# Top-k attention and a low-rank mixer: weighted values of two steps formed together at every other step, with a third buffer for transposed probabilities

## The chip, the cores and the metric

The kernel runs on one core of one Trainium2 chip. The core has five engines that run side by side: TensorE (PE, the matrix array; its weight loads are shown apart as PEld), VectorE (DVE), ScalarE (ACT), GpSimd (POOL) and SyncE (SP, which here issues the DMA transfers). The metric is the device time of one execution in microseconds. The kernel before takes 1774.49 us, the median of three runs from 1774.05 to 1775.44; the profiled execution has a span of 1773.6 us.

## The reference

Attention over 8 batches, 8 heads, 576 rows and a head dimension of 64 keeps the 32 largest scores of each row; its output goes through a low-rank mixer along the sequence and a two-layer MLP. All of it is float32.

```python
scores = scale * np.matmul(q, k.transpose(0, 1, 3, 2))
kth = np.partition(scores, -top_k, axis=-1)[..., -top_k:-top_k + 1]
scores = np.where(scores >= kth, scores, -1000000000.0)
attn = np.exp(scores - np.max(scores, axis=-1, keepdims=True))
attn = attn / (np.sum(attn, axis=-1, keepdims=True) + 1e-09)
x = np.matmul(attn, v)        # then heads side by side: (8, 576, 512)
h = x.transpose(0, 2, 1) @ U @ V
u = x + h.transpose(0, 2, 1)
out = u + np.maximum(u @ w_ch1, 0.0) @ w_ch2
```

U is 576 x 32 and V 32 x 576; w_ch1 is 512 x 2048 and w_ch2 2048 x 512.

## The kernel before

**Tiles and steps.** Heads go in pairs: 4 pairs a batch, 32 pairs g in all. The 576 rows of a pair make five chunks: t = 0 to 3 are 128 rows of both heads, and t = 4 holds the last 64 rows of both heads stacked. One chunk is one step, so step n = 5g + t runs from 0 to 159, and the loop goes on to n = 161 to finish.

**What happens to a chunk.** `scores` (L320 for t = 4, L333 otherwise) forms the scores on TensorE; ACT copies them to the tile Ssb. `front` runs on DVE: it alternates MAX8 (L385, L399) and MATCH_REPLACE8 (L395) to find the 32nd largest score. GpSimd and ACT push the smaller scores far down (L402 and L403, or L419 to L421), and `weigh` (L351) writes the exponentials to E. The chunk's E must then be turned, so that its rows lie along the free dimension, into the tile PT. `turns` does it by transposes on TensorE (L474, L479) with ACT copies (L475, L480). From chunk 30 on (`shared`), the second head of the chunks t < 4 takes another way, `blocks`: a DVE transpose of 32 x 32 blocks (L446), a DMA to DRAM (L452) and back into PT (L456). `values` (L508 and L512, or L498 for t = 4) multiplies PT by the pair's values into a PSUM tile O, which ACT copies to XT (L521), or scales into x for t = 4 (L506). In L508 the stationary operand is 128x128, with the last 64 rows of both heads on a diagonal; in L512 it is 128x64, and the two heads write the two halves of O. In L333 the two heads use the two halves of the array's rows. In L498 the stationary operand is PT itself, 128x128.

**After the last chunk of a pair.** `mixed` transposes XT (L533), applies the row sums, and forms the low-rank products (L544, L556, L558). It is a generator that goes on by one piece with each `fill()`; after the last pair of a batch it puts that batch's MLP, `mlp(b)`, into `fillers`.

**What sets the order.** The order of work on TensorE, ACT, DVE and GpSimd is the order in which the program is written; no planner moves it. In step n from 21 on, the loop issues in turn: the transposes of chunk n-2 between the first four `fill()` calls, the values of chunk n-2, the scores of chunk n+1, and four more `fill()` calls, with pieces of `front` for chunk n and `blocks` for chunk n-1 between. Each `fill()` adds a fixed share to `due` and then takes matmuls of the MLP (L581 and L600) from `fillers` until `due` is paid; if `fillers` is empty, `due` is set to zero. The share is one MLP's work spread over the calls of four head pairs, times `SHORT` in steps with t = 4, times `EARLY` up to step 42. What is left at the end of the loop is run in the last `while` loop.

```python
share = MLP_WORK / (NPAIR * SLOTS * (NT + SHORT))
due += share * (SHORT if t == NT else 1) * (EARLY if n <= 2 * ALONE + 2 else 1)
```

**Buffers.** PT has two buffers of 4.5 KB a partition. The tile hT (two ReLU outputs of one MLP part) has `HT` = 10 buffers of 2.5 KB; one part of an MLP, 320 or 256 columns, fills eight. PSUM tiles of transposes, O, and the mixer's products share a ring of two buffers, `ps_t`; scores have two in `ps_s`, MLP products two in `ps_m`.

Of the kernel before, what the change touches and what calls it, by code (L numbers as in the profile page):

```python
# [8 lines left out]
F32 = mybir.dt.float32  # L9
# [17 lines left out]
def kernel(  # L27
# [30 lines left out]
    P = 128  # L58
# [4 lines left out]
    NT, TAIL = 4, 64  # L63
# [6 lines left out]
    CH = NT + 1  # L70
    ALONE = NPAIR * CH
# [2 lines left out]
    NV = 3  # L74

    BLK = 32
    HT = 10
    PE, ACT = mybir.EngineType.PE, mybir.EngineType.Activation
    DVE, POOL = mybir.EngineType.DVE, mybir.EngineType.Pool

# [2 lines left out]
    attn = ctx.enter_context(tc.tile_pool(name="attn", bufs=2))  # L83
# [45 lines left out]
    def cols(t):  # L129
        return slice(t * P, t * P + rows(t))  # L130
# [4 lines left out]
    def half(h):  # L135
        return slice(h * D, (h + 1) * D)
# [226 lines left out]
    def eased(g, t):  # L363
        return bool(ways(g, t)[2])
# [69 lines left out]
    def shared(g, t):  # L434


        return t < NT and g * CH + t >= ROUNDED

    def blocks(g, t):


        E2 = probs[g, t]
        PT = attn.tile([P, 2 * NT + 1, P], F32, tag="PT", name="PT")
        PTs[g, t] = PT
        y = attn.tile([P, 4, NT, BLK], F32, tag="y", name="y", bufs=1)
        nc.vector.transpose(  # L446
            y.rearrange("p r c j -> p c r j"),
            E2[:, S + TAIL : 2 * S].rearrange("p (c r j) -> p c r j", c=NT, r=4),
        )
        away = dram.tile([P, 4, P], F32, tag="away", name="away")  # L450
        for a in range(4):
            nc.sync.dma_start(  # L452
                away[:, a].rearrange("(r i) n -> i r n", r=4),
                y[a * BLK : (a + 1) * BLK].rearrange("i r c j -> i r (c j)"),
            )
        nc.sync.dma_start(  # L456
            PT[:, NT : 2 * NT].rearrange("p a n -> p (a n)"), away.rearrange("p a n -> p (a n)")
        )

    def turns(g, t):  # L460


        E2 = probs.pop((g, t))
        nh = 2 if t < NT else 1
        if shared(g, t):
            PT = PTs[g, t]
        else:
            PT = attn.tile([P, 2 * NT + 1, P], F32, tag="PT", name="PT")
            PTs[g, t] = PT
        for h in range(1 if shared(g, t) else nh):  # L470
            tp = ps_t.tile([P, NT, P], F32, tag="tp", name="tp")
            for j in range(NT):
                a = h * (S + TAIL) + j * P
                nc.tensor.transpose(tp[:, j, :], E2[:, a : a + P], ident)  # L474
            nc.scalar.copy(PT[:, NT * h : NT * h + NT], tp)  # L475
            yield
        tp = ps_t.tile([P, P], F32, tag="tp", name="tp")
        a = MAIN if nh == 2 else S - P
        nc.tensor.transpose(tp, E2[:, a : a + P], ident)  # L479
        nc.scalar.copy(PT[:, NT * nh], tp)  # L480
        yield

    def inverse(g, lo, hi):
        den = dens[g][:, lo:hi]
        if g == NPAIR - 1:
            nc.vector.tensor_scalar_add(den, den, 1e-9)
        nc.vector.reciprocal(den, den)

    def values(g, t):

        PT = PTs.pop((g, t))
        va, vd, vt = (a[g % NV] for a in (vas, vds, vts))
        O = ps_t.tile([P, P], F32, tag="tp", name="O")
        if t == NT:
            den, x = dens[g], xs[g % 2]
            inverse(g, 2 * NT if g == NPAIR - 1 else 0, 2 * NT + 1)
            for j in range(NT + 1):
                nc.tensor.matmul(  # L498
                    O,
                    lhsT=PT[:, j],  # L500
                    rhs=va[:, :, j, :] if j < NT else vt,
                    start=(j == 0),
                    stop=(j == NT),
                )
            for h in range(2):
                nc.scalar.mul(x[half(h), NT, half(h)], O[half(h), half(h)], den[half(h), 2 * NT :])  # L506
            return
        nc.tensor.matmul(O, lhsT=vd, rhs=PT[:, 2 * NT], start=True, stop=False)  # L508
        PB = PT[:, NT : 2 * NT].rearrange("p a (c j) -> p c a j", c=NT) if shared(g, t) else None
        for j in range(NT):  # L510
            for h in range(2):
                nc.tensor.matmul(  # L512
                    O[half(h)],
                    lhsT=va[:, h, j, :],
                    rhs=PB[:, j] if h and shared(g, t) else PT[:, NT * h + j],
                    start=False,
                    stop=(j == NT - 1),
                )
        if t == 0:
            XTs[g] = attn.tile([P, MAIN], F32, tag="XT", name="XT")  # L520
        nc.scalar.copy(XTs[g][:, cols(t)], O)  # L521
# [49 lines left out]
    def mlp(b):  # L571
# [3 lines left out]
        for chunks, (lo, hi) in zip(PARTS, SPAN):  # L575
            w = hi - lo
            hTs = []
            for f in range(NF):
# [11 lines left out]
                if f % 2 == 0:  # L590
                    hT = mlpp.tile([P, 2, WIDE], F32, tag="hT", name="hT", bufs=HT)
                    hTs += [hT[:, 0], hT[:, 1]]
# [73 lines left out]
    STEPS = NP * CH  # L666
# [4 lines left out]
    fillers, mixing, due = [], [], 0.0  # L671
# [29 lines left out]
    for n in range(STEPS + 2):  # L701
        g, t = divmod(n, CH)
        if n < STEPS:
            if t == 0 and g + 1 < NP:
                load(g + 1)
            if t == 1 and g + 1 < NP:
                ready = prep(g + 1)
            fronts[n] = front(g, t)
            next(fronts[n])
        here, last = fronts.get(n, iter(())), fronts.pop(n - 1, iter(()))  # L710
        if n >= ALONE - 1 and n <= ALONE:

            if n < ALONE:
                next(last)
                values(*divmod(n - 3, CH))
                list(turning)
                next(here)
                next(last)
                scores(*divmod(n + 1, CH))
                values(*divmod(n - 2, CH))  # L720
            list(turns(*divmod(n - 1, CH)))
            values(*divmod(n - 1, CH))
            if n < ALONE:
                next(here)
                next(here)
                inverse(g, 0, 2 * NT)
                mixing.append(mixed(g, 1))
                fill()
                next(here)
                continue  # L730
            fill()
            scores(*divmod(n + 1, CH))
            next(here)
            while mixing:
                fill()
            next_params(1)
            fill()
            next(last, None)
            next(here)
            fill()  # L740
            next(here)
            next(here)
            fill()
            continue
        ease = eased(*divmod(n - 1, CH))
        if n < ALONE:
            if ease:
                next(last, None)
            scores(*divmod(n + 1, CH))
            if n >= 3:  # L750
                values(*divmod(n - 3, CH))
                if (n - 3) % CH == NT:
                    mixing.append(mixed((n - 3) // CH, 3))
            list(turning)
            fill()
            next(here)
            if t < NT:
                next_params(1)
            fill()
            next(ready, None)  # L760
            next(here)
            next(last, None)
            fill()
            next(here)
            if t in (0, 1):
                next_params(1)
            next(here)
            fill()
            if n >= 1:
                turning = turns(*divmod(n - 1, CH))  # L770
            continue
        away = n <= STEPS and shared(*divmod(n - 1, CH))
        if ease:
            next(last, None)
        fill()
        next(turning, None)
        fill()
        next(turning, None)
        if away:
            next(last)  # L780
        fill()
        next(turning, None)
        fill()
        if ease:
            next(last, None)
        if n - 2 >= ALONE:
            values(*divmod(n - 2, CH))
        if n + 1 < STEPS:
            scores(*divmod(n + 1, CH))
        next(here, None)  # L790
        next_params(1)
        if n - 2 >= ALONE and (n - 2) % CH == NT:
            mixing.append(mixed((n - 2) // CH, 5))
        fill()
        next(here, None)
        if away:
            blocks(*divmod(n - 1, CH))
        fill()
        if n <= STEPS:
            turning = turns(*divmod(n - 1, CH))  # L800
        fill()
        next(here, None)
        next(ready, None)
        if t in (1, 3):
            next_params(1)
        next(here, None)
        fill()
# [33 lines left out]
```

## Time and profile before

| | kernel before |
|---|---|
| median of 3 runs | 1774.49 us |
| span of the profiled execution | 1773.6 us |
| PE busy | 1669.3 us, 94% |
| DVE busy | 1560.3 us, 88% |
| ACT busy | 1029.4 us, 58% |
| POOL busy | 846.8 us, 48% |
| mean granted TensorE clock | 0.968 |
| 20 steps in the steady stage | 200.6 us |

A row of the table is the time in which an engine had at least one instruction running. Matmuls overlap, so a matmul's own duration in the profile is longer than its share of TensorE's time; what counts is the distance from one matmul's start to the next one's. The span has three parts: up to 250 us the weights are unpacked beside the first chunks; from 450 to 1620 us the steps repeat with a period of five; after 1633 us, when the last chunk is done, the rest of the MLP work runs by itself. A line of the timeline reads: start in us, length in us, engine, line, operation, output <- inputs, array shape (rows * columns used), moving operand, count, and in brackets the idle time before it with what ended it. A line of the chain of waits reads: start, length, engine, output, line, count.

### The profile page before, as it was taken

How to read it: one execution, taken by the hardware profiler on the slowest of the kernel's cores; microseconds unless marked ns; L12 is line 12 of the kernel's file. 1: busy time of each engine (PE TensorE's matmuls, PEld its weight loads, DVE VectorE, ACT ScalarE, POOL GpSimd, SP SyncE). 2: the span in 40 equal slices, each digit the busy share in tenths (PEclk: the TensorE clock that was granted, in tenths of full speed). 3: DMA queues.
4: the chain of work that ended last, by engine and by line, in shares of the span. 5: the costliest groups of instructions: out<-in, count | busy, mean ns of one | idle time of the engine just before them, and what ended most of it. 6: DMA issues, size and time to landing. Idle time of an engine off the chain costs nothing.

```text
span 1773.6 us, 28992 instructions
## 1 busy us (share of the span) xinstructions
PE 1669.3 (94%) x9851; PEld 1257.5 (71%) x9851; DVE 1560.3 (88%) x3106; ACT 1029.4 (58%) x2682; POOL 846.8 (48%) x591
## 2 busy tenths in 40 slices
PE   4666789999999999999999999999999999999999
PEld 2434556677777877788777877788777877788677
DVE  7999989899999999999999999999999999994000
ACT  4778777555656656565656656565656656564100
POOL 4777677535354554545445454444445444453000
PEclk7687799999999999999999999999999999999999
DMA  3222332222223332222233232232233232211010
GB/s 95 88 82 73 88 85 61 50 59 71 58 67 80 66 72 56 67 68 64 64 71 79 62 70 62 65 70 63 63 73 80 59 73 60 53 50 45 4 15 13
DMA packets 275829, 112.79 MB, mean 64 GB/s; under 512 B 173920, under 2 KB 260192, under 8 KB 275680
## 3 DMA queue, kind: packets, MB, share of 16 engines
q1 hardware_dynamic: 274624, 110.68, 26.4%
q8 instruction: 77, 1.26, 0.3%
q14 instruction: 72, 0.59, 0.1%
q10 hardware_dynamic: 1056, 0.26, 0.1%
HBM read 74.15 MB, written 36.70 MB: 63 GB/s over the span
## 4 chain that ended last, share of the span: by engine, by line
PE 75%; DVE 16%; POOL 4%; ACT 3%; issue 2%; DMA 1%; SPq 0%; POOLq 0%; DVEq 0%
PE mm L581 25%; PE mm L600 24%; DVE rr L395 7%; PE sc L333 6%; PE O L512 6%; DVE m L399 6%; PE tp L474 3%; DVE first L385 2%; PE sc L320 2%; PE O L498 2%; PE up L556 1%; PE O L508 1%; POOL E L402 1%; PE up L558 1%; PE tp L648 1%
## 5 line engine op out<-in xcount | busy, mean ns | idle before, releaser
L399 DVE MAX8 m<-rr 128x8 f32<-128x576 f32 x864 | 614.7, 748 | 5.5
L600 PE MATMUL mm<-hT,w 128*128 128x256 f32 (+1 forms) x2048 | 547.4, 410 | 0.0
L581 PE MATMUL mm<-uT,w 128*128 128x256 f32 (+1 forms) x2048 | 541.5, 410 | 0.9 <-ACT hT L593 0.9
L402 POOL TENSOR_SCALAR E<-Ssb,m 128x576 f32<-128x576 f32 x127 | 281.1, 2214 | 411.7 <-DVE m L399 409.1
L581 PEld LDWEIGHTS mm<-uT,w 128*128 128x128 f32 x2048 | 371.7, 190 | 115.1 <-issue 26.0
L600 PEld LDWEIGHTS mm<-hT,w 128*128 128x128 f32 x2048 | 368.3, 190 | 106.8 <-issue 22.5
L395 DVE MATCH_REPLACE8 rr<-m,rr 128x576 f32<-128x576 f32 x576 | 427.2, 742 | 0.0
L421 POOL TENSOR_TENSOR Ssb<-Ssb,E 128x576 f32<-128x576 f32 x159 | 225.4, 1418 | 122.3 <-ACT E L420 121.7
L351 ACT ACTIVATE E<-Ssb,nmax 128x576 f32<-128x576 f32 x288 | 223.3, 776 | 52.4 <-POOL Ssb L403 34.9
L593 ACT ACTIVATE hT<-mm 128x320 f32<-128x320 f32 (+1 forms) x256 | 105.1, 411 | 240.4 <-PE mm L581 240.1
L385 DVE MAX8 first<-Ssb 128x8 f32<-128x576 f32 x288 | 203.3, 742 | 31.4 <-ACT Ssb L346 31.4
L395 DVE MATCH_REPLACE8 rr<-first,Ssb 128x576 f32<-128x576 f32 x288 | 211.8, 742 | 0.0
L403 POOL TENSOR_TENSOR Ssb<-Ssb,E 128x576 f32<-128x576 f32 x127 | 179.3, 1412 | 10.6
L333 PE MATMUL sc<-qkT 64*128 64x288 f32 x1024 | 170.6, 454 | 6.7 <-ACT Ssb L344 5.8
L474 PE MATMUL tp<-ident,E 128*128 128x128 f32 x736 | 116.0, 283 | 37.1 <-ACT XT L521 14.6
L512 PE MATMUL O<-PT,va 128*64 128x128 f32 x2048 | 146.3, 284 | 1.9 <-DMA PT<-away 1.9
L474 PEld LDWEIGHTS tp<-ident,E 128*128 128x128 f32 x736 | 92.1, 145 | 68.7 <-ACT XT L521 16.6
L475 ACT COPY PT<-tp 128x512 f32<-128x512 f32 x184 | 106.6, 585 | 49.0 <-PE tp L474 46.4
L512 PEld LDWEIGHTS O<-PT,va 128*64 128x64 f32 x2048 | 113.7, 140 | 19.0 <-DMA PT<-away 2.9
L420 ACT ACTIVATE E<-Ssb,least 128x576 f32<-128x576 f32 x159 | 123.3, 776 | 5.2
L333 PEld LDWEIGHTS sc<-qkT 64*128 64x128 f32 x1024 | 93.3, 198 | 45.3 <-issue 14.3
L613 DVE TENSOR_TENSOR oT<-uT,mm 128x320 f32<-128x320 f32 (+1 forms) x8 | 3.6, 455 | 137.1 <-PE mm L600 137.1
(81 smaller groups left out, 1574.0 us busy)
## 6 DMA issues: line engine op xcount, KB each, us to landing
away<-y SPq DMA_DIRECT2D x416, 64.0 KB, 1.8
PT<-away SPq DMA_DIRECT2D x104, 256.0 KB, 2.8
raw<-in_moe_w_ch_dram SPq DMA_DIRECT2D x32, 512.0 KB, 3.8
va<-in_v_dram SPq DMA_DIRECT2D x64, 128.0 KB, 2.3
out_dram<-ob SPq DMA_DIRECT2D x57, 128.0 KB, 2.2
ld<-in_q_dram SPq DMA_DIRECT2D x108, 64.0 KB, 2.4
ld<-in_k_dram SPq DMA_DIRECT2D x108, 64.0 KB, 2.4
ld<-in_q_dram SPq DMA_DIRECT2D x108, 8.0 KB, 2.2
```

Of the source, the lines that this page charges most:

```text
L333: nc.tensor.matmul(sc[:, h, 0:HALF], lhsT=qkT[half(h), 0, cols(t)], rhs=qkT[half(h), 1, i * HALF : (i + 1) * HALF], start=True, stop=True,)
L351: nc.scalar.activation(E, chunk, AF.Exp, bias=nmax, scale=SCALE, accum_out=total)
L385: nc.vector.max(ms[c], curs[c])
L395: nc.vector.match_replace(nxt, ms[c], curs[c], NEG)
L399: nc.vector.max(ms[c], curs[c])
L402: nc.gpsimd.tensor_scalar(Es[c], chunks[c], ms[c][:, 7:8], NEG, ALU.is_lt, ALU.mult)
L403: nc.gpsimd.tensor_tensor(chunks[c], chunks[c], Es[c], ALU.add)
L421: nc.gpsimd.tensor_tensor(chunks[c], chunks[c], Es[c], ALU.subtract)
L474: nc.tensor.transpose(tp[:, j, :], E2[:, a : a + P], ident)
L512: nc.tensor.matmul(O[half(h)], lhsT=va[:, h, j, :], rhs=PB[:, j] if h and shared(g, t) else PT[:, NT * h + j], start=False, stop=(j == NT ...
L581: nc.tensor.matmul(ph[:, 0:w], lhsT=w1[:, cc, f * P : (f + 1) * P], rhs=uT[:, cc, lo:hi], start=(cc == 0), stop=(cc == NC - 1),)
L600: nc.tensor.matmul(po[:, 0:w], lhsT=w2[:, f, c * P : (c + 1) * P], rhs=hTs[f][:, 0:w], start=(f == 0), stop=(f == NF - 1),)
```

## The change

Chunks are weighted in twos. At an even step the loop now forms the values of chunks n-3 and n-2, one after the other; at an odd step it forms none. Scores keep their place, once a step, behind the values. When a pair's last chunk is odd, its `mixed` is thereby put on the list one step later. A chunk's PT now has to live one step longer, so PT gets a third buffer; HT falls from 10 to 8, which gives back the space.

```diff
-    HT = 10
+    HT = 8
...
-        PT = attn.tile([P, 2 * NT + 1, P], F32, tag="PT", name="PT")
+        PT = attn.tile([P, 2 * NT + 1, P], F32, tag="PT", name="PT", bufs=3)
...
-            PT = attn.tile([P, 2 * NT + 1, P], F32, tag="PT", name="PT")
+            PT = attn.tile([P, 2 * NT + 1, P], F32, tag="PT", name="PT", bufs=3)
...
-        if n - 2 >= ALONE:
-            values(*divmod(n - 2, CH))
+
+        weighted = [n - 2] if n > STEPS else [m for m in (n - 3, n - 2) if n % 2 == 0 and m >= ALONE]
+        for m in weighted:
+            values(*divmod(m, CH))
         if n + 1 < STEPS:
             scores(*divmod(n + 1, CH))
         next(here, None)
         next_params(1)
-        if n - 2 >= ALONE and (n - 2) % CH == NT:
-            mixing.append(mixed((n - 2) // CH, 5))
+        for m in weighted:
+            if m % CH == NT:
+                mixing.append(mixed(m // CH, 5))
```

## Prediction

> **What bounds the kernel now.** I read the page first, then the busy time by stretches, the chain of work that ended last inside one steady stretch, the waits, and last the timeline around the one place where TensorE pauses. From the page:
>
> ```profile
> PE 1669.3 (94%) x9851; PEld 1257.5 (71%) x9851; DVE 1560.3 (88%) x3106; ACT 1029.4 (58%) x2682; POOL 846.8 (48%) x591
> ...
> PE 75%; DVE 16%; POOL 4%; ACT 3%; issue 2%; DMA 1%; SPq 0%; POOLq 0%; DVEq 0%
> ```
>
> Shares over the whole span mix stages, so the next view is busy time by stretch (length, then PE, PEld, DVE, ACT, POOL; then granted clock):
>
> ```profile
> 440.00:450.00 10.00, 8.08 (x48) 5.89 (x47) 9.93 (x22) 4.84 (x14) 4.05 (x4) 0.83 0.43 102
> ...
> 700.00:900.00 200.00, 199.83 (x1215) 152.46 (x1214) 193.47 (x384) 119.57 (x318) 95.94 (x64) 1.00 0.30 67
> ```
>
> From 450 to 1620 us TensorE is busy without a gap and DVE has 3% to spare. The list of waits has none of TensorE's between 500 and 1600 us; DVE's own there are 15.9 us for score copies. So in the steady stage the time is the sum of what TensorE's instructions take, and a thing is worth only what it adds to or takes from that sum. The chain there (start, length, what; L600 is the second MLP product, L474 and L479 transposes, L508 and L512 weighted values, L333 scores):
>
> ```profile
> 913.51 0.54 PE mm L600 x2
> 914.05 0.11 PE tp L479
> 914.16 1.08 PE mm L600 x4
> 915.24 0.22 PE O L508 x2
> 915.46 1.03 PE O L512 x16
> 916.49 1.17 PE sc L333 x8
> 917.66 3.43 PE mm L600 x12
> ```
>
> Four L600 take 1.08, so one 320-column matmul 0.27 us; one of 128 columns 0.11 (L479, or L508 x2 in 0.22). L512 fills half the array's columns and runs in pairs: 16 make 8 pairs, 8 x 0.11 = 0.87, but they take 1.03. L333 fills half the rows: 4 pairs of 288 columns at 0.27 x 288/320 = 0.24 make 0.97, but they take 1.17. Twelve L600 after them should take 3.23 and take 3.43. So each group that begins or ends with another shape of array use carries 0.16 to 0.20 us extra, three times a step.
>
> **What the Trainium skill says.** "TensorEngine Tiling (Array Packing)", Tiling Modes, Key Properties: changing the tiling mode, not merely the tile, drains TensorE. The chain agrees: the extra stands where 128x128 meets 128x64, 128x64 meets 64x128, and 64x128 meets 128x128; L600 to L508, both 128x128, pays nothing. "TensorE: Matmul & The Clock Gate", Part 2, Step-by-step: weight loads are pulled ahead of running matmuls, while matmuls keep program order. That fits the 0.27 and 0.11 inside a mode, where no load shows; the part of the extra after a switch is about one load that nothing covers. Same page, Part 1: after an idle window of about 3.4 us the clock falls to half. Here a pause of 1.92 us was followed by a clock of 0.83 in the stretch above. "Perfetto Trace Analysis", Tensor Engine Instruction: matmul ends are estimated, so I used distances between starts.
>
> **The change part by part.** *Order of values.* Before, step n does V (values of n-2), then S (scores of n+1). After, an even step does V(n-3), V(n-2), S, and an odd step S alone. Products, bytes and copies stay the same. Modes, with full for 128x128: V is full (L508) then 64 columns (L512); S is row mode. Two steps before: full, col, row, full, col, row, full: 6 switches. Two steps after: full, col, **full, col**, row, full, then full, row, full: 7. The second L508 puts the array back to full width between the two L512 groups. That is one extra switch, from L512 into L508. Its price from the nearest rows: 0.16 (L512 into L333, exit and half of a short load) to 0.20 (L333 into L600, whose weights are 128 wide as L508's are). I take 0.20. For V of t=4 (L498, all full): pair (t=3, t=4) also has one extra, L512 into L498; pair (t=4, t=0) has none, as L498 to L508 keeps full mode. Even steps from 46 to 160 are 58; step 160 has no S and comes out even, and 11 are (4,0) pairs. 46 x 0.20 = **9.2 us**, all on the path, as nothing else bounds this stage. At 0.16 it is 7.4. The earlier ten pairs lie where TensorE pauses anyway (step 42, below) and are counted at nothing.
>
> *When an MLP opens.* An MLP is handed out by fill() once mixed() has finished the batch's last head pair. That pair's last V is m = 19, 39, 59 ...: always odd, so it moves from step m+2 to m+3, and every MLP from the second on opens eight fill calls later. Does the stock last? One MLP is 144 units (a unit is 512 columns of one product). A call asks 0.9677 units (0.629 for t=4): 36.0 per five steps, and 0.91 of it up to step 42. From step 20: four calls 3.5, steps 21 to 24 25.7, steps 25 to 39 98.3, steps 40 and 41 14.1: 141.6. The rest, 2.4, is gone in the third call of step 42. mixed() needs nine calls from its first. Before, these are calls 5 to 8 of step 41 and 1 to 5 of step 42: the stock is dry for two calls. The timeline shows just that:
>
> ```profile
> 441.12 0.65 PE L600 MATMUL mm<-hT,w 128*128 128x256 f32 x2
> 443.69 0.44 PE L648 MATMUL tp<-ident,oT 128*128 128x128 f32 x2 [1.92 <-POOL oT L616]
> ...
> 448.70 4.57 PE L581 MATMUL mm<-uT,w 128*128 128x320 f32 x16
> ```
>
> After, it is dry until call 5 of step 43: four calls of 0.881 and four of 0.968 more, 7.4 units. fill() forgets this debt, so the work goes to the end of the program. A unit is 1.08/(2 x 0.625) = 0.86 us: **6.4 us** move to the tail. From step 43 on, 20 steps ask 144 units and an MLP opens every 20 steps, so this happens once. Not all of it is lost, since TensorE can use the room to run ahead. Its transposes of step 45 start at 470.15 now. After, those of step 44 can't start before their weights E, written at 457.11 at the end of a chain through DVE that fill() doesn't feed; from there to step 45's transposes lie 0.55 transposes, 3.35 + 2.5 + 0.8 fillers, 3.2 for two V and 1.2 S: 11.6, so 468.7. It runs 1.5 us ahead, and 4.9 are lost. If ACT, with fewer copies to serve, writes E 2 us sooner, 2.9 are lost; if a second half-clock window falls on real work, 1.7 more. I take **4.7**. In the tail, TensorE waits 1.3 us for POOL between the last two MLPs (1643 us); the moved units cover most of it: **-1.0**.
>
> *Third buffer and HT = 8, which pays for it.* Nothing for either. PT(n-1) takes the buffer of PT(n-4), last read a step or more before. With eight hT tiles, a new first ReLU must wait for the last part's readers of that tile; but those L600 stand ahead of the L581 that the ReLU waits for, and TensorE keeps order.
>
> *Waits moved.* S for even n comes some 1.4 us earlier against the rest, S for odd n at its old place; DVE waits only for scores at t=0, so it gains nothing that bounds. Transposes of even m come 1.4 us earlier: they start 3 to 6 us after E is written, so none waits. PT of even m keeps its place, PT of odd m gets a step more. Behind a delayed XT copy on ACT stand S copies, and behind these only DVE, which has its 3%.
>
> Sum: 9.2 + 4.7 - 1.0 = 12.9, and half a microsecond for the clock: 1774.5 + 13.5 = **1788**.
>
> **The rivals.** (1) *Switches alone*: the run-ahead absorbs the dry calls and the half clock falls on idle time. For: transposes have up to 7 us of slack in steps 43 and 44. Against: one step later it is 4 to 5. 1774.5 + 9.2 - 1.0 = 1783. (2) *A new wait*: the uneven pairs make T533 wait for the XT copy of t=3, now 2.5 us before it rather than a step, or L508 for copies that ACT serves late. For: ACT is late by 1 us with such copies at times. Against: 2.5 covers that. With 0.5 us in each of 70 pairs, half of it lost: 1788 + 17 = 1805. (3) *Not slower*: the entry into the second L508 is covered by loads pulled ahead, and the pairs remove waits before 500 us. For: TensorE's waits from 250 to 500 us sum to 10.7, among them 1.5 for a PT copy. Against: every switch now in the trace pays. Switch nothing, dry calls 4.7, less half of 10.7: 1774.
>
> **How the numbers follow.** Forecast 0.68, rival 1 0.14, rival 2 0.08, rival 3 0.10. The range runs from 0.16 a switch with nearly all of the dry calls hidden (7.4 + 1, 1782) to 0.20 on all 56 pairs with every dry call lost and two half-clock windows (11.2 + 6.4 + 3.4, 1795), leaving rivals 2 and 3 out. Slower 0.91 (forecast, rivals 1 and 2), the tenth of rival 3 split about its 1774: faster 0.05, same 0.04.
>
> **What would show it.** Right: per 20 steady steps 1.6 us more TensorE time (200.6 now); L512 into the second L508 about 0.10 late and that L508 pair about 0.10 long; a TensorE gap of several us near 440 to 460; the tail after the last V longer by some 5 us. Wrong: L508 starting straight after L512, new TensorE waits for ACT in even steps, or no more idle time at 440 us than now.

## The result and the profile after

The changed kernel takes 1788.37 us (median of 4 runs, 1788.18 to 1789.83), the kernel before 1774.65. The ratio is 1.0079, with a 95% interval from 1.0061 to 1.0096: it is slower by some 14 us. The forecast was 1788.

The page of the changed kernel, in the lines that answer to those shown of before:

```profile
PE 1674.6 (94%) x9851; PEld 1248.1 (70%) x9851; DVE 1560.2 (87%) x3106; ACT 1025.6 (57%) x2682; POOL 846.6 (47%) x591
...
PE 52%; DVE 25%; POOL 9%; issue 7%; ACT 4%; DMA 1%; SPq 1%; POOLq 0%; DVEq 0%; ACTq 0%
```

TensorE has as many matmuls as before and DVE is busy for as long, yet the span is 12.9 us longer. Shares by engine tell nothing about it: the time lies between the matmuls. Busy time by stretch (length, then PE, PEld, DVE, ACT, POOL; then granted clock):

```profile
430.00:440.00 10.00, 5.92 (x31) 4.73 (x29) 9.93 (x21) 4.97 (x14) 5.18 (x4) 0.91 0.28 71
440.00:450.00 10.00, 7.36 (x56) 6.12 (x56) 9.75 (x21) 5.33 (x15) 2.51 (x4) 0.75 0.39 88
...
700.00:900.00 200.00, 199.76 (x1211) 150.45 (x1210) 192.15 (x383) 119.41 (x320) 94.86 (x64) 1.00 0.29 66
```

In the steady stage TensorE is as full as before, but 200 us hold less of the kernel: its matmuls fall from 1215 to 1211 and DVE's busy time from 193.5 to 192.2. Around 440 us there is now a real hole. The timeline of TensorE in one even step (start, length, engine, line, operation, output <- inputs, array shape, moving operand, count) shows the first of the two costs:

```profile
903.50 1.78 PE L581 MATMUL mm<-uT,w 128*128 128x320 f32 x6
905.12 0.38 PE L508 MATMUL O<-PT,vd 128*128 128x128 f32 x2
905.43 1.09 PE L512 MATMUL O<-PT,va 128*64 128x128 f32 x16
906.45 0.49 PE L508 MATMUL O<-PT,vd 128*128 128x128 f32 x2
906.87 1.09 PE L512 MATMUL O<-PT,va 128*64 128x128 f32 x16
907.90 1.19 PE L320 MATMUL sc<-qkT 64*64 64x288 f32 x8
```

Read the starts, not the lengths. From the first L508 to its L512 it is 0.31 us, from the second L508 to its L512 0.42: the same two matmuls take 0.11 more, because the array has to come back from half width. From either L512 group to what follows it, it is 1.02 or 1.03, whether an L508 or the scores follow, so nothing is added there. The other 0.09 stands in the odd step, where the scores now follow the MLP's full-width matmuls directly:

```profile
895.66 1.24 PE L581 MATMUL mm<-uT,w 128*128 128x320 f32 x4
896.83 1.24 PE L333 MATMUL sc<-qkT 64*128 64x288 f32 x8
```

Four L581 take 4 x 0.27 = 1.08 where an L508 follows, and 1.17 here. Together the two parts make the price of 0.20. The prediction read it from the chain of waits, whose pieces run from one end to the next; there it stands at other groups, but the sum is the same.

The second cost is the hole. Around the end of the first MLP, where the kernel before waited 1.92 us at L648 (its lines are in the prediction), the changed kernel shows:

```profile
435.32 0.60 PE L600 MATMUL mm<-hT,w 128*128 128x256 f32 x2
440.98 0.69 PE L648 MATMUL tp<-ident,oT 128*128 128x128 f32 x2 [5.07 <-POOL oT L616]
441.46 1.91 PE L498 MATMUL O<-va,PT 128*128 128x128 f32 x8
...
449.52 0.62 PE L544 MATMUL pT<-x,U 128*32 128x128 f32 x10 [1.66 <-POOL x L538]
...
453.44 4.58 PE L581 MATMUL mm<-uT,w 128*128 128x320 f32 x16
```

With nothing left in the stock, the turning back of the MLP's last output (L648) comes straight after its last matmul and waits 5.07 us for GpSimd, and the values and scores queued behind it wait along. The half clock that follows makes L498 take 1.91 for eight, where they took 1.05 in the kernel before at 1632 us.

To see where the 14 us lie I used the starts of the scores of chunks 21, 45, 85, 145 and 159, which mark the same place in the work in every kernel. All columns are us; "end" is the end of the span.

| kernel | to 21 | 21 to 45 | 45 to 159 | of it 85 to 145 | 159 to end |
|---|---|---|---|---|---|
| before | 214.1 | 252.1 | 1142.1 | 600.37 | 165.3 |
| changed | 211.4 | 251.6 | 1151.6 | 605.79 | 171.8 |
| changed_again | 213.0 | 250.7 | 1151.6 | 605.81 | 171.8 |
| buffers_only | 212.7 | 249.1 | 1142.0 | 600.43 | 165.2 |
| mixed_late_only | 211.4 | 254.8 | 1145.2 | 602.75 | 171.7 |
| pairs_at_odd | 213.3 | 253.6 | 1151.4 | 605.62 | 166.8 |
| batch_end_on_time | 212.7 | 249.6 | 1150.4 | 605.12 | 165.2 |
| pairs_late_only | 212.3 | 254.5 | 1150.3 | 605.12 | 165.4 |
| pairs_early_only | 212.9 | 251.1 | 1142.6 | 601.60 | 165.2 |
| corner_last | 212.8 | 252.4 | 1159.3 | 609.84 | 165.5 |
| corners_together | 213.9 | 250.0 | 1142.5 | 601.66 | 171.4 |
| corners_on_time | 212.9 | 249.2 | 1141.8 | 600.27 | 164.9 |
| corners_load_later | 214.1 | 248.6 | 1140.6 | 599.69 | 164.9 |

The first column differs by up to 3 us between kernels that are the same up to there: that is the scatter of one execution, and with it comes part of the second. Half-clock stretches between 200 and 450 us fall in different places from run to run. The later columns repeat within 0.1 in the two profiles of the changed kernel. The kernel before takes 200.12 per 20 steps from 85 to 145; the 200.6 given for it above holds only for stretches of 20 steps that begin before step 70.

### The profile page after: what moved, and what is told of

Same layout as the page of the kernel before. It is cut to its first block, busy times and chain, and to the rows that moved or that the text cites. A ratio compares the mean times of both kernels' runs of the same rounds, so it can differ in the third digit from the quotient of the medians.

```text
span 1786.4 us, 28987 instructions
## 1 busy us (share of the span) xinstructions
PE 1674.6 (94%) x9851; PEld 1248.1 (70%) x9851; DVE 1560.2 (87%) x3106; ACT 1025.6 (57%) x2682; POOL 846.6 (47%) x591
## 4 chain that ended last, share of the span: by engine, by line
PE 52%; DVE 25%; POOL 9%; issue 7%; ACT 4%; DMA 1%; SPq 1%; POOLq 0%; DVEq 0%; ACTq 0%
PE mm L581 18%; PE mm L600 17%; DVE rr L395 11%; DVE m L399 9%; PE sc L333 4%; PE O L512 4%; DVE first L385 3%; POOL E L402 3%; POOL Ssb L421 2%; PE tp L474 2%; POOL Ssb L403 2%; PE up L556 1%; PE O L508 1%; ACT E L351 1%; PE sc L320 1%
## 5 line engine op out<-in xcount | busy, mean ns | idle before, releaser
L581 PE MATMUL mm<-uT,w 128*128 128x256 f32 (+1 forms) x2048 | 541.3, 410 | 3.2 <-ACT hT L593 3.2
L581 PEld LDWEIGHTS mm<-uT,w 128*128 128x128 f32 x2048 | 372.0, 190 | 114.9 <-issue 23.2
L351 ACT ACTIVATE E<-Ssb,nmax 128x576 f32<-128x576 f32 x288 | 223.2, 776 | 91.5 <-POOL Ssb L403 64.5
L421 POOL TENSOR_TENSOR Ssb<-Ssb,E 128x576 f32<-128x576 f32 x159 | 225.0, 1415 | 95.2 <-ACT E L420 95.0
L512 PE MATMUL O<-PT,va 128*64 128x128 f32 x2048 | 142.3, 281 | 1.6 <-DMA PT<-away 1.6
L512 PEld LDWEIGHTS O<-PT,va 128*64 128x64 f32 x2048 | 110.9, 138 | 17.9 <-issue 2.7
```

The source lines that it names most:

```text
L351: nc.scalar.activation(E, chunk, AF.Exp, bias=nmax, scale=SCALE, accum_out=total)
L421: nc.gpsimd.tensor_tensor(chunks[c], chunks[c], Es[c], ALU.subtract)
L512: nc.tensor.matmul(O[half(h)], lhsT=va[:, h, j, :], rhs=PB[:, j] if h and shared(g, t) else PT[:, NT * h + j], start=False, stop=(j == NT ...
L581: nc.tensor.matmul(ph[:, 0:w], lhsT=w1[:, cc, f * P : (f + 1) * P], rhs=uT[:, cc, lo:hi], start=(cc == 0), stop=(cc == NC - 1),)
```

## The experiments

Each was timed in five rounds beside the kernel before; ratios are to it, with their 95% intervals.

**The buffers alone.** The kernel before, with

```diff
-    HT = 10
+    HT = 8
-        PT = attn.tile([P, 2 * NT + 1, P], F32, tag="PT", name="PT")
+        PT = attn.tile([P, 2 * NT + 1, P], F32, tag="PT", name="PT", bufs=3)
```

at both places of PT.

> The kernel before with HT = 8 and the third PT buffer, order of work as before. Theory (all of the time comes from TensorE's mode switches and from the MLP stock running dry): 1774.5, within 1.5 us of before. Rival (part of it is a wait on the smaller hT ring, or on where the tiles lie): 1777 or more, with waits of ACT or TensorE in the MLP groups.

1774.90, ratio 1.0003 (0.9994 to 1.0011). The buffers cost nothing and give nothing by themselves.

**The later mixer alone.** The kernel before, with

```diff
-        if n - 2 >= ALONE and (n - 2) % CH == NT:
-            mixing.append(mixed((n - 2) // CH, 5))
+        for m in [n - 2] if n > STEPS else [m for m in (n - 3, n - 2) if n % 2 == 0 and m >= ALONE]:
+            if m % CH == NT:
+                mixing.append(mixed(m // CH, 5))
```

> The kernel before, with mixed() put on the list at the same step as in the changed kernel, values every step as before. Theory: every MLP from the second on opens eight fill calls later, the stock runs dry once, 6.4 us of products move to the tail and 5 to 6.4 of them are lost: 1780 (1778.5 to 1781.5), steady 20 steps still 200.6. Rival (the dry calls are absorbed by running ahead, and the switches are all of the change): 1774.5 to 1776.

1784.87, ratio 1.0058 (1.0045 to 1.0071): slower by 10 us, twice what was expected. The rival, that nothing is lost, falls. The tail is 6.4 us longer, as the theory has it; but the stretch from 21 to 45, which should have become shorter by some of the work that left it, became longer. Among TensorE's waits, by the list for 205 to 1650 us:

```profile
PE tp L648 <- POOL oT L616: 4.0, 1, 4.0
PE O L512 <- DMA PT<-away: 3.6, 5, 2.7
...
PE O L508 <- ACT uT L566: 2.0, 1, 2.0
```

The first is the wait of the hole above, and the third falls into the steps just after it, at 455 us. Of the second, 2.8 us lie in this stretch. So the loss is more than the moved products: the hole adds waits of its own, and TensorE doesn't run ahead. The steady stage is longer too, by 2.4 us in 60 steps, where I expected no change. By the starts, 2.0 of these stand at V (L512, which waits for the DMA of PT, and the scores behind it) and 0.4 ahead of L544, whose PSUM tile ACT still reads (L650).

**Pairs at odd steps.** The changed kernel, with

```diff
-        weighted = [n - 2] if n > STEPS else [m for m in (n - 3, n - 2) if n % 2 == 0 and m >= ALONE]
+        weighted = [m for m in (n - 3, n - 2) if n % 2 == 1 and m >= ALONE]
```

> The changed kernel, with the pairs at odd steps instead of even ones, so that the last chunk of a batch, always odd, is weighted as early as before. Theory: the extra switches stay (about 9.5 us), the dry calls go: 1783 (1781 to 1785), 202.2 to 202.4 per 20 steady steps. Rival (the uneven load of paired steps costs, not the opening of the MLP): 1788, as the changed kernel.

1788.86, ratio 1.0082 (1.0069 to 1.0095): by its time alone the rival won. Its profile says otherwise for the part in question. The tail after the last values is 140.4 us as before, against 146.7 in the changed kernel, and 60 steady steps take 605.62. But the stretch from 21 to 45 takes 253.6, against 251.6 and 250.7 in the changed kernel's two profiles. Two of its waits are longer there than with even pairs, where the first is 3.2 and 1.2 us and the second isn't listed:

```profile
PE mm L581 <- ACT hT L593: 3.9, 3, 3.0
PE tp L533 <- ACT x L506: 3.2, 1, 3.2
```

Moving the pairs by a step changes more than the opening of the MLP, so this run didn't separate the two costs. The following one does.

**The batch's last chunk on time.** The changed kernel once more, and the changed kernel with

```diff
-        weighted = [n - 2] if n > STEPS else [m for m in (n - 3, n - 2) if n % 2 == 0 and m >= ALONE]
+        weighted = [
+            m for m in (n - 3, n - 2)
+            if m >= ALONE and (m == n - 2 if m % ALONE == ALONE - 1 else n % 2 == 0)
+        ]
```

> The changed kernel once more, for a second profile and more times beside the next three. Every theory: 1788.4, within 1 us.

> The changed kernel, except that a batch's last chunk (19, 39, 59 ...) is weighted alone at its odd step, as early as before, so the MLP opens on time. Its pair was one without an extra switch, so TensorE's mode switches stay as many as in the changed kernel. Theory (the dry calls cost some 4.9 us: 6.4 us moved to the tail, less what the stretch before step 45 gets shorter): 1783.5 (1782 to 1785), tail after the last values 140.3 us as before, 202.2 per 20 steady steps. Rival (moving products to the tail costs nothing net, since pairs_at_odd without dry calls took 1788.9): 1787.5 to 1789.

1788.84 (ratio 1.0078, 1.0064 to 1.0092) and 1781.30 (ratio 1.0035, 1.0023 to 1.0048). The rival falls: an MLP that opens one step late costs 7.5 us. That is more than the 4.9 of the theory, and 1781.30 lies below its range. The two profiles differ by 9.2, scatter at the start included: 6.5 after 159, 1.2 between 45 and 159, 1.1 between 21 and 45 and 0.3 before. The 6.5 of products that left the stretch from 21 to 45 gained nothing there. With the mixer on time, the wait for GpSimd is the shorter one of before,

```profile
440.79 0.44 PE L648 MATMUL tp<-ident,oT 128*128 128x128 f32 x2 [2.14 <-POOL oT L616]
...
444.30 4.57 PE L581 MATMUL mm<-uT,w 128*128 128x320 f32 x16
```

and this kernel's profile has no half clock there, nor L544's wait of 1.7 us for GpSimd. The changed kernel's longer wait at L648 (2.9), its wait at L544 (1.7) and its 6.8 us at half clock (at most 3.4) make 8.0, enough for the 6.5 + 1.1 = 7.6 that the stretch lost. What remains of the change costs 6.7 us. In 60 steady steps it is 605.12 - 600.37 = 4.75, and these hold 24 pairs with an extra switch: 0.198 each.

**Pairs in one part alone.** The same kernel, with pairs only from chunk 43 on (`or m < 43` behind the test for the batch's last chunk), or only up to chunk 42 (`or m > 42`):

> batch_end_on_time with pairs from chunk 43 on alone; the chunks up to 42 are weighted every step as before. Theory (the pairs cost 46 switches of 0.198 us after step 45, and gain some 2.5 us before it, where they spare TensorE two waits for PT at step 34): the cost without the gain, 1774.6 + 9.1 = 1783.7 (1782.5 to 1785). Rival (the early pairs gain nothing, the steady ones cost less than 0.198): 1781.3 as batch_end_on_time, or less.

> batch_end_on_time with pairs up to chunk 42 alone; every chunk after is weighted at its own step as before. Theory: the gain without the cost, 1774.6 - 2.4 = 1772.2 (1771 to 1773.5), 200.6 per 20 steady steps. Rival (early pairs only add their switches, some 1.6 us): 1775 to 1776.5.

1784.12 (1.0049, 1.0036 to 1.0061) and 1773.11 (0.9991, 0.9983 to 0.9999). Both came as the theory has it: pairs in the steady stage cost 9.6 us, and pairs before it gain, 2.8 us by the first comparison (1784.12 against 1781.30) and 1.4 by the second, whose interval all but touches no change. A difference that the theory named shows at step 34. In the kernel with pairs in the late part alone (before, the same two waits are 1.02 and 1.72):

```profile
361.33 0.49 PE L508 MATMUL O<-PT,vd 128*128 128x128 f32 x2 [1.25 <-ACT PT L480]
...
363.95 1.97 PE L512 MATMUL O<-PT,va 128*64 128x128 f32 x14 [1.77 <-DMA PT<-away]
```

And with pairs in the early part alone:

```profile
360.26 1.09 PE L512 MATMUL O<-PT,va 128*64 128x128 f32 x16
361.29 0.49 PE L508 MATMUL O<-PT,vd 128*128 128x128 f32 x2
361.70 0.43 PE L512 MATMUL O<-PT,va 128*64 128x128 f32 x2
362.55 1.09 PE L512 MATMUL O<-PT,va 128*64 128x128 f32 x14 [0.41 <-DMA PT<-away]
```

The older chunk's values are ready and fill the time in which the newer one's PT is copied and lands; 2.6 us of waiting go, and the half clock after them as well (L512 x14 in 1.97 against 1.09). That this is where the gain comes from is not shown. Over the whole stretch from 21 to 45, TensorE's listed waits sum to 14.6 us in pairs_early_only and 14.2 in batch_end_on_time, against 13.0 before and 15.5 in pairs_late_only, so elsewhere waits grew. What differs more is the half clock: 3.4 us and none, against 10.2 in each of the two others. How much of that belongs to the early pairs, and how much to the scatter of these stretches, one profile of each can't tell.

The 60 steps of pairs_early_only take 1.2 us more than before, which wasn't expected. All of it stands in one place: at 1313 us an L512 waits 0.82 us for the DMA of PT.

**The price of a switch by itself.** The kernel before, no pairs, L508 behind the L512 of its own O:

```diff
-        nc.tensor.matmul(O, lhsT=vd, rhs=PT[:, 2 * NT], start=True, stop=False)
...
-                    start=False,
-                    stop=(j == NT - 1),
+                    start=(j == 0),
+                    stop=False,
                 )
+        nc.tensor.matmul(O, lhsT=vd, rhs=PT[:, 2 * NT], start=False, stop=True)
```

> The kernel before, with L508, which uses the full array, moved behind the eight half-width L512 of the same O: no pairs, and nothing else is moved. Each of these V then has one more change of mode (full, half width, full, row instead of full, half width, row). Theory (an entry into the full mode costs 0.198 us): 16 such V in 20 steady steps make 200.6 + 3.2 = 203.8, 92 of them after step 45 make 18.2, and up to 3 us before it: 1794 (1791 to 1798). Rival (the 0.198 belongs to a pair's second O, not to the mode): 1774.6 to 1777.

1792.43, ratio 1.0100 (1.0085 to 1.0116). The chain in the steady stage (start, length, what; L511 is the half-width group here, L518 the full one):

```profile
910.07 1.62 PE mm L600 x6
911.69 1.02 PE O L511 x16
912.71 0.42 PE O L518 x2
913.13 1.12 PE sc L320 x8
```

L518 x2 takes 0.42, where L508 x2 took 0.22 ahead of the group. 60 steps take 609.84 - 600.37 = 9.47 longer and hold 48 such V: 0.197 each. The same products, the same accumulation and no pair: the price belongs to the change of mode, not to a second O.

**The pair regrouped.** The changed kernel, with a pair's full-width matmuls first:

```diff
+    def corner(g, t):
+        O = ps_t.tile([P, P], F32, tag="tp", name="O")
+        nc.tensor.matmul(O, lhsT=vds[g % NV], rhs=PTs[g, t][:, 2 * NT], start=True, stop=False)
+        return O
...
         for m in weighted:
-            values(*divmod(m, CH))
+            if m % CH == NT:
+                values(*divmod(m, CH))
+        begun = [(m, corner(*divmod(m, CH))) for m in weighted if m % CH < NT]
+        for m, O in begun:
+            values(*divmod(m, CH), O)
```

where `values` leaves out its own L508 when it is given an O. Then the same with the batch's last chunk on time, and that with the loads a step later.

> The changed kernel, with the pair's matmuls regrouped: first all that use the full array (L498 for a chunk t = 4, and the L508 of both chunks), then the half-width L512 of both. No product is added or removed. Theory: two switches fewer than the changed kernel in 34 pairs and one fewer in 12, at 0.20 each 16 us: 1772.5 (1770.5 to 1774.5), the dry calls still there, 199 to 199.4 per 20 steady steps. Rival (the extra in the second L508 is the price of a pair's second accumulation or of its PT, not of the mode): 1785 or more.

> corners_together with the batch's last chunk on time. Theory: 4.9 us less than corners_together's 1779.2, so 1774.3 (1772.5 to 1776). Rival (nothing net from the dry calls): 1779.

> corners_on_time with the next pair's loads issued a step later (after blocks of step t = 1 instead of at t = 0, and its turning on DVE at t = 2), so that the DMA of PT isn't queued behind them. Theory (with fewer mode switches TensorE arrives at PT before its DMA has landed, 3.1 us in 6 waits and more, and the loads hold that DMA up): those waits go, 3 us less than corners_on_time, 1771 (1769.5 to 1773). Rival (the DMA is late because DVE is, which is now the bound): no change.

1779.18 (1.0028, 1.0017 to 1.0040), 1771.31 (0.9979, 0.9970 to 0.9988) and 1769.87 (0.9974, 0.9964 to 0.9985). The regrouping gives back 9.7 us of the changed kernel's and 10.0 with the batch's end on time, not 16. In the last kernel, L492 is the full-width group and L521 the half-width one:

```profile
901.05 0.44 PE O L492 x4
901.50 1.90 PE O L521 x32
903.39 1.12 PE sc L320 x8
```

L521 x32 takes 1.90 where two groups of 16 took 1.02 each: one entry into half width saves 0.14, not 0.20, so a regrouped pair saves 0.34, and the sum is 34 x 0.34 + 12 x 0.20 = 14. The rest went into new waits. The kernel with the batch's end on time has, from 460 to 1610 us,

```profile
PE O L492 <- ACT ob L661: 2.4, 6, 0.4
PE pT L553 <- issue: 0.8, 2, 0.6
```

since a pair that opens two O at once needs both tiles of the ring. In the 60 steps the sum by prices is 18 x 0.34 + 6 x 0.20 = 7.3 and the measured gain 605.12 - 600.27 = 4.85; by the starts, 2.0 of the rest stands at the second L492 of six pairs and 0.7 ahead of L553. That is why 20 steady steps take 200.1 to 200.6 and not 199 to 199.4. Opening the MLP on time is worth 7.9 us here, again more than 4.9.

The third kernel's loads were aimed at waits for the DMA of PT. From 460 to 1610 us these were 1.6 us in corners_together's profile and none in the second kernel's, so that theory wasn't put to the test. Whether the 1.4 us between the two are real stays open, as their intervals overlap; five of the third's seven runs lie below all ten of the second's, and in its profile the wait at L553 is gone. Both beat the kernel before.

## Why the prediction came out right

The total was right, 1788 against 1788.37, and each of its two causes is shown by a run that takes it away. That it is right to half a microsecond is luck: two terms were off, by 3.8 us and by 1.4 to 2.8, in opposite directions.

- *TensorE bounds the steady stage.* Right: 24 and 48 added switches lengthened 60 steps by 4.75 and 9.47, the same price each. It isn't bound by TensorE's work alone everywhere: the late mixer by itself (2.4 us) and the regrouped pairs (2.5 us) brought waits into these 60 steps. The forecast of 1.6 more per 20 steps came out as 1.8, of which 1.6 are switches.
- *One extra switch a pair, 0.20 us, 9.2 in all.* Right in kind and size. 0.198 and 0.197 by two independent runs; the steady pairs cost 9.6 us by pairs_late_only. The Trainium skill's page "TensorEngine Tiling (Array Packing)", Tiling Modes, says that a change of mode drains; here, by the starts, leaving a mode takes 0.09 (0.31 from L508 to L512, less 2 x 0.11), and entering one 0.11 more into 128x128 (0.42 against 0.31) and some 0.06 into 128x64 (1.02 less 0.87 and 0.09). That the second part is a weight load that nothing covers is the prediction's reading and wasn't tested.
- *The stock runs dry once, and 6.4 us move to the tail.* Right: 6.5 by the table.
- *TensorE runs 1.5 us ahead, so 4.7 are lost, and the tail hides 1.0.* This is the step that failed in size: the net of 3.7 was forecast, and 7.5 were lost. I held TensorE back only by the weights E of the following chunks. What held it was L648, which stands in its queue ahead of the values and waited 5.07 us instead of 1.92. In the second profile of the changed kernel the reason can be followed:

```profile
438.83 0.78 ACT L351 ACTIVATE E<-Ssb,nmax 128x576 f32<-128x576 f32 x1 [1.55 <-POOL Ssb L403]
439.61 0.35 ACT L615 COPY oT<-mm 128x256 f32<-128x256 f32 x1
```

```profile
438.76 1.41 POOL L421 TENSOR_TENSOR Ssb<-Ssb,E 128x576 f32<-128x576 f32 x1
440.12 0.72 POOL L616 TENSOR_TENSOR oT<-oT,uT 128x256 f32<-128x256 f32 x1
```

ACT's copy for it (L615) stands behind the exponential of that step (L351), which waits for GpSimd, and GpSimd adds (L616) only after the masking (L421). The half clock that came with that pause was a further loss. And the tail's wait of 1.3 us stayed, because that L648 too comes straight after its MLP's last matmul, with the moved products ahead of it and none beside it:

```profile
1657.56 0.44 PE L648 MATMUL tp<-ident,oT 128*128 128x128 f32 x2 [1.32 <-POOL oT L616]
```

- *The early pairs count at nothing.* Wrong by 1.4 to 2.8 us in the kernel's favour, by the two runs above. Rival 3 had named waits before 500 us that pairs remove, but took this together with free switches. (The waits that it sums to 10.7 are 10.9 by the list.)
- *Third buffer and HT = 8 at nothing.* Right.
- *New waits (rival 2).* L533 and L648 behind the scores start 0.15 to 0.17 us later than usual, eleven times from 45 to 159; by the table the late mixer costs 1.2 us in that stretch. Real, but far from 17.

By medians: 9.6 for steady pairs, -2.8 for early ones and 7.5 for the late MLP make 14.3, against 14.2 measured for changed_again. This is no check of the parts, since each is the difference of two kernels that follow each other on the way from before to changed, and such differences add up whatever their causes. An independent sum is 46 x 0.198 = 9.1, with -1.4 and 7.5: 15.2. In another order the late mixer alone cost 10. By the profiles it loses 3.1 from 45 to 159, against 1.2 within the change, where odd chunks' PT have a step more to land; that this is the reason wasn't tested.

## What to carry to other kernels

When one engine is full, list the order of its instructions by mode before and after a change, and count the borders; a grouping that looks tidier can have more of them, and the same grouping one level deeper, full-width work first, has fewer. When a change delays the moment at which background work becomes ready, check whether the stock lasts until then, and look at what stands at the head of the queue when it doesn't: here everything on TensorE behind L648 waited for that, not for its own inputs.

## What the runs showed of the hardware

The price of a change of mode depends on what is entered: 0.198 us into 128x128 with float32 weights (4.75 us for 24 entries, 9.47 for 48), and about 0.14 for a group less in 128x64.

The clock fell after pauses that differ in length, and not after every one. Before, L648's pause of 1.92 us was followed by 3.4 us of half clock; in the changed kernel one of 5.07 us came with 6.8. But pauses of 2.11 and 2.14 us at the same L648, in the profiles of buffers_only and batch_end_on_time, were followed by none. So the length of a pause alone doesn't decide it; the window of about 3.4 us that the prediction sets beside the 1.92 isn't a limit here.

Such stretches move from run to run. From 21 to 45, the profile of the kernel before has 10.2 us of half clock and takes 252.1, that of buffers_only 3.4 and 249.1; these 3.0 us are most of the 4.5 between their spans. The times of buffers_only spread from 1770.89 to 1776.07; how much of that is clock, one profile can't show.
